# A V copy, a V cast and the folding of two weight matrices reordered, in a kernel of sliding-window attention and a multiplicative FFN

## The chip, the cores and the metric

The kernel runs on one core of one Trainium2 chip. The metric is the device time of one execution in microseconds (us), median of several runs. The engines are named as in the profile: PE (matmuls; PEld is its loading of weights), DVE (vector), ACT (scalar), POOL (GpSimd) and SP (which here only issues DMAs). POOL issues DMAs too, between its own instructions.

## What is computed

q, k and v are (8 batches, 8 heads, 576 positions, 64), fp32. Attention is causal with a window of 64 positions; its output, 4608 tokens of 512 values, goes through an FFN that multiplies two projections and has two output matrices with nothing between them:

```python
scores = scale * np.matmul(q, k.transpose(0, 1, 3, 2))
mask = (rel >= 0) & (rel < window)          # rel = query - key, window = 64
attn = softmax(where(mask, scores, -1e9))
x = (attn @ v).transpose(0, 2, 1, 3).reshape(4608, 512)
a = x @ w1; b = x @ w2                      # 512 x 1024 each
out = (a * b @ w3) @ w_out                  # 1024 x 1024, then 1024 x 512
```

## The kernel before, in words

Everything is computed in fp16 with fp32 accumulation. The order of all instructions is written out by hand: each engine works through its own list in program order, and semaphores join the lists.

**Folding.** Since nothing stands between w3 and w_out, the kernel computes wc = w3 @ w_out once and uses that. w3 has eight row blocks of 128 (`fc` 0 to 7). `fold_t(fc)` (L487) turns one with eight PE transposes (L492) into a PSUM bank `f_ps`, and DVE copies it back over the block (L493). `fold_mm(fc, half, cp, nf)` (L495) multiplies `nf` turned blocks with one half (256 columns) of w_out, eight matmuls for each block (L501), and `cp` copies the result to `wc_sb` (L503). Blocks 0 to 3 lie in the tile `ab` and blocks 4 to 7 in a part of `xT` that the first batches don't use. Before, all first halves are done as their blocks are turned, and the second halves of two blocks at a time follow between the values of batch 0.

**Loads at the start.** q and k of batch 0 come through the queues of SP and ACT. All else is on POOL's queue, which converts to fp16 on the way: w3 in four pieces of two blocks (`load_w3(n)`, L482, 512 KB read each), w_out in two halves (`load_wo(half)`, L476, 512 KB each), V of batch 0 (`load_rows(0, "v")`, L217, two of 288 KB), then w1 and w2 in halves (L471), k and q of batch 1, and V of batch 1 in blocks (`load_v`, L241).

**V.** Batch 0's V comes in rows, is cast into another order in two halves (`cast_qk`, L226), transposed (`transposes`, L262 on PE with copies L266) and transposed back per block of keys (`keys_of_v`, L273 and L275). From batch 1 on V is loaded by blocks of 128 keys straight into `v16s[b % 2]`, blocks 0, 2, 3 and parts of 4 and 5; block 1 and half of 4 overlap others and are copied from them on DVE by `copy_v(b, c)` (L245, L247).

**Attention.** A batch has six steps d (three segments of 192 queries, two pairs of heads). `scores(d)` is 8 matmuls into the bank `s_ps` (L296), an exp on ACT (L300), and two masks on POOL (L308 and L310; four in the first segment). `values(d)` is 16 matmuls with V into `o_ps`, or into `s_ps` if that is given (L338; L354 from batch 2 on), a logarithm and an exp on ACT (L344, L345) for the reciprocal of the sums, and a multiply on DVE (L346) into `xT`. Batch 1's steps are d = 6 to 11.

**FFN.** `ffn_ab(g, fc)` is 16 matmuls of 128x512 into two banks `f_ps` (L432), a copy on ACT (L437) and a multiply on DVE (L438), for 512 tokens `g` and a column block `fc`. `ffn_o(g, t)` is eight matmuls with `wc_sb` for 128 tokens (L450), a copy on DVE (L452) and a store on SP's queue (L459). There are three `f_ps` banks, one `o_ps`, one `s_ps` (of two banks each) and one `tp`.

**The order around the change** is L540 to L660: loads, casts and transposes of batch 0, scores(0) to scores(5) among the first fold steps, V of batch 0, values(0) to values(5) among the other fold steps, then batch 1's k and q: cast (half on DVE, half on ACT) and transposed. From `ffn_ab(0, 0)` (L624) on, FFN work of the first 512 tokens stands between the steps of batch 1; POOL casts batch 2's k and q in the same stretch (L634, L638) and issues the loads of its V (L639, L651). From L676 on a planner places later work by due times; it isn't touched. `keep_busy(n)` (L523) is n matmuls without use.

Of the kernel before, what the change touches and what calls it, by code (L numbers as in the profile page):

```python
# [8 lines left out]
FP32 = mybir.dt.float32  # L9
# [6 lines left out]
P = 128  # L16
# [128 lines left out]
def kernel(  # L145
# [11 lines left out]
    nc = tc.nc  # L157
    B, H, S, D = q.shape
    N = B * S
    DM = H * D  # L160
# [52 lines left out]
    def load_rows(b, which):  # L213

        t = sb.tile([P, 2, TI * D], FP16, name="rows", bufs=3)
        for hh in range(2):
            nc.gpsimd.dma_start(out=t[:, hh], in_=big_rows(which, b, hh))  # L217
        raws[which, b] = t
# [6 lines left out]
    def cast_qk(b, which, hh, cp):  # L225
        cp(t16_of(b, which)[:, :, hh * D:hh * D + D], raws[which, b][:, hh].rearrange("p (i d) -> p i d", d=D))  # L226
# [16 lines left out]
    def copy_v(b, c):  # L243
        vh = v_heads(b)
        dve_cp(vh[0:D, c], vh[D:P, c - 1])  # L245
        if c == 1:
            dve_cp(vh[D:P, 1], vh[0:D, 2])  # L247
# [4 lines left out]
    def transposes(b, which, *cs, into=None, cps=None):  # L252

        t16 = t16s[which, b]
        if cs[0] == 0:
            turned[which, b] = sb.tile([P, NJ, S], FP16, name=which + "T", bufs=1 if which == "v" else 2)
        dst = turned[which, b]
        if into is None:
            into = [ps_t.tile([P, 6, P], FP16, name="tp")]
        for c, tp in zip(cs, into):  # L260
            for i in range(6):
                nc.tensor.transpose(tp[:, i, :], t16[:, 6 * c + i, :], ident16)  # L262
        if cps is None:
            cps = [dve_cp if which == "k" or c != 1 else act_cp for c in cs]
        for c, tp, cp in zip(cs, into, cps):
            cp(dst.rearrange("q j (p i) -> q j p i", i=TI)[:, :, :, 6 * c:6 * c + 6],  # L266
               tp.rearrange("q i (p j) -> q j p i", p=TP))

    def keys_of_v(b, js, into, cps):

        for j, tp in zip(js, into):
            for c in range(6):
                nc.tensor.transpose(tp[:, c, :], turned["v", b][:, j, VBLK[c]:VBLK[c] + P], ident16)  # L273
        for j, tp, cp in zip(js, into, cps):
            cp(v16s[b % 2][:, :, j].rearrange("p c (a e) -> p c a e", a=2)[:, :, :, 0:D],  # L275
               tp.rearrange("p c (a e) -> p c a e", a=2))
# [37 lines left out]
    def values(d, pool=None):  # L314
        b, r = divmod(d, 6)
        si, jp = divmod(r, 2)
        j0 = 2 * jp
        v16 = v16s[b % 2]
        pt = probs.pop(d)
        seg = SEGS[si]  # L320
        q_base = seg[0][1]
        o_ps = ps_v.tile([P, 2, 512], FP32, name="o_ps") if pool is None else \
            ps_s.tile([P, 2, 512], FP32, name="s_ps")
        if jp == 0:
            lns[b, si] = sb.tile([P, NJ, 192], FP32, name="ln_s", bufs=4)
        y = lns[b, si][:, j0:j0 + 2]
        r = sb.tile([P, 2, 192], FP32, name="r")
        x0 = (b * S + q_base) % RING
        xs = xT[:, j0:j0 + 2, x0:x0 + 192]
        if b < SHORT:  # L330

            for jj in range(2):
                c0 = 0
                for bi, (k0, q0, n, _) in enumerate(seg):
                    o0 = jj * 192 + q0 - q_base
                    for e in range(2):
                        for a in range(2):
                            nc.tensor.matmul(o_ps[a * D:a * D + D, e, o0:o0 + n],  # L338
                                             v16[:, si * 2 + bi, j0 + jj, (2 * a + e) * D:(2 * a + e) * D + D],
                                             pt[:, a, jj, c0:c0 + n],  # L340
                                             start=(jj == 0 and bi == 0), stop=(bi == 1), skip_group_check=True)
                    c0 += n
            o, total = (o_ps[:, e, 0:384].rearrange("p (j n) -> p j n", j=2) for e in range(2))
            nc.scalar.activation(y, total, AF.Ln)  # L344
            nc.scalar.activation(r, y, AF.Exp, scale=-1.0)  # L345
            nc.vector.tensor_tensor(xs, o, r, ALU.mult)  # L346
            return
        for jj in range(2):
            first = True
            for a in range(2):  # L350
                c0 = 0
                for bi, (k0, q0, n, _) in enumerate(seg):
                    o0 = a * 192 + q0 - q_base
                    nc.tensor.matmul(o_ps[:, jj, o0:o0 + n],  # L354
                                     v16[:, si * 2 + bi, j0 + jj, a * D:a * D + P],
                                     pt[:, a, jj, c0:c0 + n],
                                     start=first, stop=(bi == 1), skip_group_check=True)
                    first = False
                    c0 += n
        nc.scalar.activation(y[0:D], o_ps[D:P, :, 0:192], AF.Ln)  # L360
        nc.scalar.activation(y[D:P], o_ps[0:D, :, 192:384], AF.Ln)  # L361
        nc.scalar.activation(r, y, AF.Exp, scale=-1.0)  # L362
        nc.vector.tensor_tensor(xs[0:D], o_ps[0:D, :, 0:192], r[0:D], ALU.mult)  # L363
        nc.vector.tensor_tensor(xs[D:P], o_ps[D:P, :, 192:384], r[D:P], ALU.mult)  # L364
# [109 lines left out]
    def load_wo(half):  # L474
        cols = slice(half * 256, half * 256 + 256)
        nc.gpsimd.dma_start(out=wo16[:, :, cols], in_=moe_w_out[:, cols].rearrange("(e p) m -> p e m", p=P))  # L476
# [7 lines left out]
    def turned_w3(fc):  # L484
        return w3_rows(fc).rearrange("p a (e n) -> p (a e) n", n=P)

    def fold_t(fc, cp=dve_cp):  # L487

        w3 = turned_w3(fc)
        tp = ps_f.tile([P, 8, P], FP16, name="f_ps")  # L490
        for ec in range(8):
            nc.tensor.transpose(tp[:, ec, :], w3[:, ec, :], ident16)  # L492
        cp(w3, tp)  # L493

    def fold_mm(fc, half, cp, nf=1):  # L495

        cols = slice(half * 256, half * 256 + 256)
        o_ps = ps_f.tile([P, 2, 256], FP32, name="f_ps")
        for f in range(nf):
            for ec in range(8):  # L500
                nc.tensor.matmul(o_ps[:, f], turned_w3(fc + f)[:, ec, :], wo16[:, ec, cols],  # L501
                                 start=(ec == 0), stop=(ec == 7), skip_group_check=True)
        cp(wc_sb[:, fc:fc + nf, cols], o_ps[:, 0:nf])  # L503
# [19 lines left out]
    def keep_busy(n):  # L523

        d = ps_t.tile([P, P], FP32, name="tp")
        for _ in range(n):
            nc.tensor.matmul(d, ident16, ident16, start=True, stop=True)
# [13 lines left out]
    load_wo(0)  # L541
    load_w3(1)
    load_rows(0, "v")
    for n in range(2, 4):
        load_w3(n)
    load_wo(1)

    def bank(pool, name):

        t = pool.tile([P, 2, 1024] if name != "f_ps" else [P, 1, 1024], FP16, name=name)  # L550
        return t[:, 0, 0:768].rearrange("p (i n) -> p i n", i=6)

    def tp_bank():
        return ps_t.tile([P, 6, P], FP16, name="tp")
# [25 lines left out]
    fold_t(2)  # L580
    fold_t(3)
    scores(4)
    fold_mm(2, 0, act_cp)
    for hh in range(2):
        cast_qk(0, "v", hh, dve_cp)
    fold_mm(3, 0, act_cp)
    scores(5)
    load_rows(1, "q")
    for i in range(2):
        load_w12(i, 1)  # L590
    load_v(1, 0, 2, 3)
    keep_busy(6)
    transposes(0, "v", 0, 1, 2, into=[bank(ps_v, "o_ps"), tp_bank(), bank(ps_f, "f_ps")], cps=[dve_cp, act_cp, act_cp])
    fold_t(4)
    fold_t(5)
    keys_of_v(0, [0, 1, 2], [bank(ps_v, "o_ps"), tp_bank(), bank(ps_f, "f_ps")], [act_cp, dve_cp, dve_cp])
    fold_mm(4, 0, act_cp)
    keys_of_v(0, [3], [tp_bank()], [dve_cp])
    fold_t(6)
    fold_mm(5, 0, act_cp)  # L600
    values(0)
    fold_t(7)
    fold_mm(6, 0, act_cp)
    values(1, ps_s)
    fold_mm(7, 0, act_cp)
    values(2)
    fold_mm(0, 1, dve_cp, 2)
    values(3, ps_s)
    fold_mm(2, 1, dve_cp, 2)
    values(4)  # L610
    fold_mm(4, 1, dve_cp, 2)
    values(5, ps_s)
    cast_qk(1, "k", 0, dve_cp)
    cast_qk(1, "k", 1, act_cp)
    load_v(1, 4, 5)
    fold_mm(6, 1, dve_cp, 2)
    cast_qk(1, "q", 0, dve_cp)
    cast_qk(1, "q", 1, act_cp)
    for n in range(3):
# [13 lines left out]
    for hh in range(2):  # L633
        cast_qk(2, "k", hh, pool_cp)  # L634
    ffn_ab(0, 4)
    scores(8)
    for hh in range(2):
        cast_qk(2, "q", hh, pool_cp)  # L638
# [3 lines left out]
    for d in range(6, 12):  # L642
        steps.pop(0)()
        store()
        if d in (6, 8):
            copy_v(1, {6: 1, 8: 4}[d])
        if d < 9:
            scores(d + 3)
        values(d, ps_s if d in (9, 11) else None)
        if d == 6:  # L650
            load_v(2, 4, 5)  # L651
        if d > 8:
            transposes(2, "k", d - 9)
# [76 lines left out]
```

## Time and profile before

| what | value |
|---|---|
| median of 6 runs | 291.99 us (291.1 to 292.8) |
| the profiled execution | 293.7 us |
| its span, first to last instruction | 292.0 us |
| PE / PEld busy | 276.2 us (95%) / 161.4 us (55%) |
| DVE / ACT / POOL busy | 180.2 (62%) / 170.0 (58%) / 179.1 (61%) |
| granted TensorE clock, mean | 0.998 |
| POOL's DMA queue (software_dynamic) | 38960 packets, 38.1% of 16 engines |

All of the stages share the 292 us, so a share of busy time says little about one of them. A timeline lists instructions of one engine, neighbours of one line merged: start and duration in us, engine, line, operation, output<-inputs, shape, count, and in brackets the idle time of the engine ahead of it with what ended it. The releaser is inferred: among several things waited for, it is the one that ended last.

### The profile page before, as it was taken

How to read it: one execution, taken by the hardware profiler on the slowest of the kernel's cores; microseconds unless marked ns; L12 is line 12 of the kernel's file. 1: busy time of each engine (PE TensorE's matmuls, PEld its weight loads, DVE VectorE, ACT ScalarE, POOL GpSimd, SP SyncE). 2: the span in 40 equal slices, each digit the busy share in tenths (PEclk: the TensorE clock that was granted, in tenths of full speed). 3: DMA queues.
4: the chain of work that ended last, by engine and by line, in shares of the span. 5: the costliest groups of instructions: out<-in, count | busy, mean ns of one | idle time of the engine just before them, and what ended most of it. 6: DMA issues, size and time to landing. Idle time of an engine off the chain costs nothing.

```text
span 292.0 us, 6234 instructions
## 1 busy us (share of the span) xinstructions
PE 276.2 (95%) x2425; PEld 161.4 (55%) x2425; DVE 180.2 (62%) x277; ACT 170.0 (58%) x281; POOL 179.1 (61%) x214
## 2 busy tenths in 40 slices
PE   7789999978998999999999999999999999999992
PEld 7668775434554555555555787455555445444441
DVE  0557456356767568687687856587867555555531
ACT  2656556664566746866776565487568765641300
POOL 8789830799469948695779363786596444402200
PEclk9999999999999999999999999999999999999999
DMA  6999999919297939094739560950094011002013
GB/s 244 222 211 204 210 205 149 399 33 112 106 334 177 64 143 327 4 113 130 311 25 126 168 237 0 168 62 2 36 154 41 2 73 73 2 36 109 2 39 112
DMA packets 48449, 37.68 MB, mean 129 GB/s; under 512 B 34160, under 2 KB 38512, under 8 KB 48416
## 3 DMA queue, kind: packets, MB, share of 16 engines
q0 software_dynamic: 38960, 11.14, 38.1%
q1 hardware_dynamic: 9024, 24.79, 23.3%
q10 hardware_dynamic: 432, 1.31, 1.3%
q8 instruction: 20, 0.33, 0.4%
q14 instruction: 13, 0.11, 0.1%
HBM read 38.80 MB, written 9.44 MB: 165 GB/s over the span
## 4 chain that ended last, share of the span: by engine, by line
PE 77%; POOL 9%; DMA 5%; ACT 4%; DVE 2%; issue 1%; SPq 0%; POOLq 0%; ACTq 0%
PE f_ps L432 36%; PE f_ps L450 20%; PE o_ps L354 5%; PE tp L262 5%; PE s_ps L296 4%; PE f_ps L501 4%; DMA ab<-in_moe_w_out_dram 3%; DMA stage<-in_q_dram 2%; POOL pt L310 2%; POOL pt L308 2%; POOL v L536 2%; POOL q L226 1%; ACT pt L300 1%; POOL v L241 1%; PE s_ps L338 1%
## 5 line engine op out<-in xcount | busy, mean ns | idle before, releaser
L432 PE MATMUL f_ps<-xT,w_sb 128*128 128x512 f16 (+1 forms) x640 | 134.2, 358 | 0.0
L308 POOL TENSOR_SCALAR_AFFINE_SELECT pt<-pt 128x512 f16<-128x512 f16 (+1 forms) x64 | 52.4, 819 | 69.7 <-ACT pt L300 69.7
L432 PEld LDWEIGHTS <-w_sb 128*128 128x128 f16 x640 | 59.7, 98 | 50.3 <-issue 0.3
L450 PE MATMUL f_ps<-wc_sb,ab 128*128 128x512 f16 (+1 forms) x296 | 66.9, 373 | 0.1
L438 DVE TENSOR_TENSOR ab<-f_ps,a_sb 128x512 f16<-128x512 f32 x72 | 49.8, 691 | 22.9 <-PE f_ps L432 21.1
L300 ACT ACTIVATE pt<-s_ps 128x1024 f16<-128x1024 f32 (+1 forms) x48 | 45.7, 952 | 23.8 <-PE s_ps L296 22.3
L437 ACT COPY a_sb<-f_ps 128x512 f32<-128x512 f32 x72 | 41.7, 579 | 24.8 <-PE f_ps L432 23.9
L310 POOL TENSOR_SCALAR_AFFINE_SELECT pt<-pt 128x512 f16<-128x512 f16 (+1 forms) x64 | 51.9, 811 | 4.5
L363 DVE TENSOR_TENSOR xT<-o_ps,r 64x384 f16<-64x384 f32 x36 | 19.8, 550 | 40.8 <-ACT r L362 40.8
L450 PEld LDWEIGHTS <-ab 128*128 128x128 f16 x296 | 27.6, 98 | 27.6 <-issue 0.3
L360 ACT ACTIVATE ln_s<-o_ps 64x384 f32<-64x384 f32 x36 | 17.5, 487 | 33.3 <-PE o_ps L354 33.3
L452 DVE COPY t2k<-f_ps 128x512 f32<-128x512 f32 (+1 forms) x36 | 24.5, 682 | 10.9 <-PE f_ps L450 10.4
L241 POOL DMA_DIRECT2D v<-in_v_dram x35 | 29.6, 853 | 2.2 <-DMA rows<-in_k_dram 1.0
L354 PEld LDWEIGHTS <-v 128*128 128x128 f16 x288 | 18.2, 98 | 9.5 <-ACT pt L300 0.8
L354 PE MATMUL o_ps<-pt,v 128*128 128x128 f16 (+1 forms) x288 | 20.8, 215 | 1.2 <-POOL pt L310 1.2
L296 PEld LDWEIGHTS <-kT 64*128 64x128 f16 x384 | 10.7, 94 | 18.1 <-issue 16.9
L364 DVE TENSOR_TENSOR xT<-o_ps,r 64x384 f16<-64x384 f32 x36 | 20.2, 561 | 0.5
L362 ACT ACTIVATE r<-ln_s 128x384 f32<-128x384 f32 x36 | 18.8, 522 | 1.1
L296 PE MATMUL s_ps<-qT,kT 64*128 64x128 f16 (+1 forms) x384 | 18.2, 214 | 0.4
L266 DVE COPY kT<-tp 128x768 f16<-128x768 f16 x19 | 18.1, 950 | 0.0
L361 ACT ACTIVATE ln_s<-o_ps 64x384 f32<-64x384 f32 x36 | 17.4, 482 | 0.4
L226 POOL CAST k<-stage 128x1152 f16<-128x1152 f32 x12 | 13.7, 1147 | 1.7 <-PE tp L262 1.7
(86 smaller groups left out, 234.2 us busy)
## 6 DMA issues: line engine op xcount, KB each, us to landing
out_dram<-t2k SPq DMA_DIRECT2D x35, 256.0 KB
stage<-in_k_dram SPq DMA_DIRECT2D x13, 576.0 KB
stage<-in_q_dram SPq DMA_DIRECT2D x13, 576.0 KB
v<-in_v_dram POOLq DMA_DIRECT2D x28, 128.0 KB, 4.5
w_sb<-in_moe_w_dram POOLq DMA_DIRECT2D x4, 512.0 KB, 12.6
ab<-in_moe_w_dram POOLq DMA_DIRECT2D x2, 512.0 KB, 8.6
ab<-in_moe_w_out_dram POOLq DMA_DIRECT2D x2, 512.0 KB, 13.5
xT<-in_moe_w_dram POOLq DMA_DIRECT2D x2, 512.0 KB, 15.1
```

What stands on the lines that cost most here:

```text
L241: nc.gpsimd.dma_start(out=vh[lo:P, c], in_=v[b, :, s0:s0 + P - lo, :].rearrange("h s d -> s h d"))
L296: nc.tensor.matmul(s_ps[:, a, jj, c0:c0 + n], kT[half, j, k0:k0 + P], qT[half, j, q0:q0 + n], start=True, stop=True, skip_group_check=True)
L300: nc.scalar.activation(pt[:, :, :, 0:w], s_ps[:, :, :, 0:w], AF.Exp, bias=-SHIFT, scale=scale)
L308: nc.gpsimd.affine_select(out=sl, in_=sl, pattern=pat, compare_op=ALU.is_ge, fill=0.0, base=off, channel_multiplier=-1)
L310: nc.gpsimd.affine_select(out=sl, in_=sl, pattern=[[-s, m] for s, m in pat], compare_op=ALU.is_ge, fill=0.0, base=63 - off, channel_multip ...
L354: nc.tensor.matmul(o_ps[:, jj, o0:o0 + n], v16[:, si * 2 + bi, j0 + jj, a * D:a * D + P], pt[:, a, jj, c0:c0 + n], start=first, stop=(bi = ...
L364: nc.vector.tensor_tensor(xs[D:P], o_ps[D:P, :, 192:384], r[D:P], ALU.mult)
L432: nc.tensor.matmul(d[:, f * n + c0:f * n + c1], w[:, dc, (fc + f) * P:(fc + f + 1) * P], xT[:, dc, xc:xc + c1 - c0], start=first, stop=(dc ...
L437: act_cp(a_sb[:, 0:nf * n], a_ps[:, 0:nf * n])
L438: nc.vector.tensor_tensor(ab[:, fc:fc + nf, lo:hi], b_ps[:, 0:nf * n].rearrange("p (f n) -> p f n", f=nf), a_sb[:, 0:nf * n].rearrange("p ...
L450: nc.tensor.matmul(o_ps[:, 0:c1 - c0], ab[:, fc, t * P:t * P + P], wc_sb[:, fc, c0:c1], start=(fc == 0), stop=(fc == 7))
L452: cp(o_sb[:, c0:c1], o_ps[:, 0:c1 - c0])
```

## The change

Three groups of edits, all in the order written out by hand.

1. `copy_v(1, 1)` moves from behind ffn_ab(0, 5) to behind ffn_ab(0, 4), ahead of scores(8).
2. V of batch 0: half 0 is cast on DVE as before, half 1 on ACT instead of DVE, and `keep_busy(6)` ahead of its transposes goes. The copies of fold_mm(2, 0) and fold_mm(3, 0) move from ACT to DVE, behind the casts.
3. The second half of w_out is loaded ahead of w3's last two pieces. Blocks 0 to 3 are folded in halves as before, but their second halves stand earlier, among V's transposes. Blocks 4 to 7 are folded at full width by a new function, `fold_full`: eight matmuls of 128x512 and one copy in place of two times eight of 128x256. The places of fold_t(4) to fold_t(7) move, and no fold step stands behind values(5) any more.

```diff
+    def fold_full(fc, cp):
+
+        o_ps = ps_f.tile([P, DM], FP32, name="f_ps")
+        for ec in range(8):
+            nc.tensor.matmul(o_ps, turned_w3(fc)[:, ec, :], wo16[:, ec, :], start=(ec == 0), stop=(ec == 7))
+        cp(wc_sb[:, fc, :], o_ps)
+
...
     load_rows(0, "v")
+    load_wo(1)
     for n in range(2, 4):
         load_w3(n)
-    load_wo(1)
...
     scores(4)
-    fold_mm(2, 0, act_cp)
-    for hh in range(2):
-        cast_qk(0, "v", hh, dve_cp)
-    fold_mm(3, 0, act_cp)
+    cast_qk(0, "v", 0, dve_cp)
+    cast_qk(0, "v", 1, act_cp)
+    fold_mm(2, 0, dve_cp)
+    fold_mm(3, 0, dve_cp)
     scores(5)
...
-    keep_busy(6)
     transposes(0, "v", 0, 1, 2, into=[bank(ps_v, "o_ps"), tp_bank(), bank(ps_f, "f_ps")], cps=[dve_cp, act_cp, act_cp])
+    fold_mm(0, 1, dve_cp, 2)
+    keys_of_v(0, [0, 1, 2], [bank(ps_v, "o_ps"), tp_bank(), bank(ps_f, "f_ps")], [act_cp, dve_cp, dve_cp])
     fold_t(4)
+    keys_of_v(0, [3], [tp_bank()], [dve_cp])
+    fold_mm(2, 1, act_cp, 2)
+    values(0)
     fold_t(5)
-    keys_of_v(0, [0, 1, 2], [bank(ps_v, "o_ps"), tp_bank(), bank(ps_f, "f_ps")], [act_cp, dve_cp, dve_cp])
-    fold_mm(4, 0, act_cp)
-    keys_of_v(0, [3], [tp_bank()], [dve_cp])
+    fold_full(4, dve_cp)
+    values(1, ps_s)
+    fold_full(5, dve_cp)
     fold_t(6)
-    fold_mm(5, 0, act_cp)
-    values(0)
+    values(2)
     fold_t(7)
-    fold_mm(6, 0, act_cp)
-    values(1, ps_s)
-    fold_mm(7, 0, act_cp)
-    values(2)
-    fold_mm(0, 1, dve_cp, 2)
     values(3, ps_s)
-    fold_mm(2, 1, dve_cp, 2)
+    fold_full(6, dve_cp)
     values(4)
-    fold_mm(4, 1, dve_cp, 2)
+    fold_full(7, dve_cp)
     values(5, ps_s)
     cast_qk(1, "k", 0, dve_cp)
     cast_qk(1, "k", 1, act_cp)
     load_v(1, 4, 5)
-    fold_mm(6, 1, dve_cp, 2)
     cast_qk(1, "q", 0, dve_cp)
...
     ffn_ab(0, 4)
+    copy_v(1, 1)
     scores(8)
...
-        if d in (6, 8):
-            copy_v(1, {6: 1, 8: 4}[d])
+        if d == 8:
+            copy_v(1, 4)
```

## The prediction

> **What bounds the kernel now.** I read the page first: PE is busy 95% of the span and DVE, ACT and POOL about 60% each, so a gain must be a hole in PE's row, and a hole counts only if nothing behind it is late as well. So I went to the places where PE stands still in the two stretches that the change edits: folding w3 and w_out (16.7 to 43.7 us) and the first FFN stage (43.7 to 89.5). In the order of PE's timeline:
>
> ```profile
> 23.17 0.51 PE L527 MATMUL tp<-ident 128*128 128x128 f16 x6
> ...
> 26.17 0.51 PE L273 MATMUL o_ps<-ident,vT 128*128 128x128 f16 x6 [0.39 <-ACT vT L266]
> ...
> 32.67 1.05 PE L501 MATMUL f_ps<-ab,xT 128*128 128x256 f16 x8 [0.44 <-DVE xT L493]
> ...
> 40.91 0.64 PE L338 MATMUL s_ps<-pt,v 128*64 128x128 f16 x16
> 41.48 1.92 PE L501 MATMUL f_ps<-ab,xT 128*128 128x256 f16 x16
> 43.74 0.50 PE L262 MATMUL o_ps<-ident,k 128*128 128x128 f16 x6 [0.34 <-ACT k L226]
> ...
> 60.19 0.43 PE L338 MATMUL o_ps<-pt,v 128*64 128x64 f16 x12 [2.15 <-DVE v L247]
> ...
> 68.27 0.64 PE L338 MATMUL s_ps<-pt,v 128*64 128x128 f16 x16 [0.22 <-POOL pt L310]
> ...
> 72.08 0.64 PE L338 MATMUL o_ps<-pt,v 128*64 128x128 f16 x16 [1.01 <-DVE t2k L452]
> ```
>
> Start, duration, and in brackets the idle time and its releaser. The change aims at three of these holes (0.39, 0.44 and 2.15 us) and at a filler (L527). Below I measure PE from start to start of its groups, because the ends of matmuls overlap what follows by about 0.1 us; so measured, the holes at 26.17, 32.67 and 43.74 are 0.52, 0.50 and 0.41 us.
>
> The last two rows matter most. In POOL's timeline behind them, from the first mask of batch 1 on:
>
> ```profile
> 52.36 0.63 POOL L308 TENSOR_SCALAR_AFFINE_SELECT pt<-pt 128x512 f16<-128x512 f16 x1 [12.13 <-ACT pt L300]
> ...
> 56.66 2.23 POOL L226 CAST k<-stage 128x1152 f16<-128x1152 f32 x2
> 58.85 1.15 POOL L308 TENSOR_SCALAR_AFFINE_SELECT pt<-pt 128x1024 f16<-128x1024 f16 x1
> 60.06 1.10 POOL L310 TENSOR_SCALAR_AFFINE_SELECT pt<-pt 128x1024 f16<-128x1024 f16 x1
> 61.11 2.23 POOL L226 CAST q<-stage 128x1152 f16<-128x1152 f32 x2
> 63.28 2.65 POOL L241 DMA_DIRECT2D v<-in_v_dram  x3
> 65.92 1.13 POOL L308 TENSOR_SCALAR_AFFINE_SELECT pt<-pt 128x1024 f16<-128x1024 f16 x1
> 67.12 1.09 POOL L310 TENSOR_SCALAR_AFFINE_SELECT pt<-pt 128x1024 f16<-128x1024 f16 x1
> ```
>
> No row after the first has an idle time: POOL is busy without a hole from 52.36 to 74.24. Its masks for scores(9) end at 68.21 and for scores(10) at 72.03, just when PE starts values(9) and values(10); the releaser named at 72.08 (a copy ending at 72.04, which values(10) doesn't read) only ended 0.01 us later. From 51 to 72 us POOL sets the end, not PE. From 72.08 to 88.08 PE has no hole.
>
> **Step 1: copy_v(1, 1) sooner.** Two DVE copies (L245 0.72, L247 1.07 us), no DMA, no added instruction. They stand one slot earlier, behind the multiply of ffn_ab(0, 4) that ends at 56.13, not behind that of ffn_ab(0, 5) at 58.28. What they read landed by 48.3 (V blocks issued at 33.8 and 35.24, landing 13.2 and 13.0 us later). They end near 58.0 before the shift of step 4; values(6) is due at 57.74, so of the 2.15 us PE keeps about 0.2. Queued behind them on DVE is the multiply of ffn_ab(0, 5), 0.4 us later; its PSUM bank is needed again only by ffn_ab(0, 7), some 2 us on. Then PE runs 2 us ahead, does values(6) to values(8) and ffn_o(0, 0), and stops at values(9), whose mask POOL still ends at 68.21. The wait moves to 68.27 and grows there from 0.22 to about 2.3 us. **Worth at the end: 0.** POOL's list is the same, and it gets no earlier unless scores(6) does.
>
> **Step 2: the fold, to the start of transposes(1, "k") (43.74).** Terms start to start, changes only:
> - keep_busy(6) goes: −0.54 (23.17 to 23.71). V's second half is now cast on ACT, behind exp(4): 22.07 plus 1.14 (ACT's row of this shape at 42.55) plus 0.06 to PE gives 23.27, so 0.10 of it becomes a wait: **−0.44**. DVE's cast of half 0 ends at 22.38 as before. exp(5), behind the ACT cast, starts at 23.28 in both; the copies of fold_mm(2) and (3) go to DVE, whose 0.9 us hole before 24.25 hides them.
> - The wait for vT at 26.17 goes, as fold_mm(0, 1) now stands there: **−0.52**. The one at 32.67 (a w3 copy queued on DVE behind a values multiply) goes too: **−0.50**. Next late is fold_full(5): its fold_t(5) copy ends near 32.9, PE comes at 33.2.
> - Rows 4 to 7 at full width: before, first halves 0.87+0.96+0.97+0.98 and second halves 2x1.85, 7.48 in all. A 128x512 group of eight took 1.81 ahead of values (73.00 to 74.81) and 1.73 ahead of transposes (75.73 to 77.46); three of one and one of the other make 7.16: **−0.32**. That fold_mm(0, 1) stands ahead of transposes and fold_t(6), (7) ahead of values gives −0.12 and +0.07: **−0.05**.
> - w_out's second half: DMA issues are moved on POOL's queue, none added, and they end at the same 12.6 us. V's rows landed at 21.91, then w3 2.48 and 2.51 us later each, w_out's half after 2.64 (11.64 plus 17.9, 29.54). In the new order the half lands at 24.55; PE, through with V's transposes at 24.28, waits **+0.27**. The w3 pieces land at 27.05 and 29.54, needed at 27.3 and 34.9: hidden. keys_of_v(3) waits 0.03 for a bank.
> - **The tail.** In before, values(5) starts at 40.91 and the k transposes 2.83 us later, because they wait for work queued on ACT behind values(5):
>
> ```profile
> 41.59 0.49 ACT L344 ACTIVATE ln_s<-s_ps 128x384 f32<-128x384 f32 x1 [1.38 <-PE s_ps L338]
> 42.12 0.52 ACT L345 ACTIVATE r<-ln_s 128x384 f32<-128x384 f32 x1
> 42.55 1.14 ACT L226 COPY k<-rows 128x1152 f16<-128x1152 f16 x1
> ```
>
> There fold_mm(6, 1) covered 1.85 of it, leaving 0.41 idle. After the change nothing of the fold stands behind values(5); ACT's three instructions are the same, so PE idles 2.26: **+1.85**, which gives back most of what was saved above.
>
> Sum: −0.44 −0.52 −0.50 −0.32 −0.05 +0.27 +0.03 +1.85 = **+0.32 us**; the transposes start at 44.06. The terms saved were real work or waits, but the fold's last piece was the cover of an ACT chain, and it is gone.
>
> **Step 3: what the rest makes of it.** ffn_ab(0, 0) to scores(6) have no hole in before and follow 0.32 later; POOL's run and values(10) too, and the q load that SP issues behind the stores at 79.05 and that POOL's cast at 86.14 waits for.
>
> **Step 4: sum.** The profiled execution took 293.7 us, span 292.0; by this it would be 294.0 and 292.3. The median shown, 291.99, lies 1.7 below that execution; moved by the same 0.32 it gives **292.3**.
>
> **Unknowns.** The w_out half in its new place: its wait is 0 if it lands by 24.28 and 1.12 if it takes what the first half took (13.13 to 16.62, 3.49); I take 2.64, the same transfer with the same queue behind it: −0.27/+0.85. The ACT cast lies between DVE's 0.45 alone and 1.35 beside POOL: −0.10/+0.21. The four wide groups may lose the 0.08 of their hand-over three times: −0.24. DVE copies beside POOL: a mask took 1.31, not 1.10, beside L226 at 23.3, but the POOL cast beside L245 at 58.31 kept its 1.14; I take 0, from 0 to +0.4 on POOL's run, and nothing below, since its rows beside L245 and L247 are within 0.05 of the others.
>
> [...] After the 2.15 us hole at 58 the next eight matmuls took 1.90, as before it, and the page's granted clock stays 9. [...] Beside POOL's work the two copies of 64x512 took 0.72 and 1.07, against 0.29 at 79.65. [...]
>
> **Rivals.** (a) The 2.15 us come off the end, since the waits list them as PE's longest in this stretch: 291.99+0.32−2.15 = 290.2. Against it stands POOL's unbroken row; it needs POOL to get quicker by itself. 0.11. (b) Slower: the w_out half lands as late as the first did, at 25.40. It decides from 24.28 on, one for one, because from there to values(5) PE's list has no other hole: +1.17, 293.2. For it: PE waited 0.66 on the first half at 16.66. Against: that one shared the engines with the q and k loads before 10 us. 0.17. (c) The change doesn't do what it says: the copies stretch to 1.1 each beside POOL's casts and values(6) still waits up to 0.7. That costs nothing while POOL decides: 292.3, inside the forecast.
>
> **Chances.** The forecast with (c), 291.4 to 292.9: 0.68. Rival (b) 0.17, (a) 0.11, and 0.04 for POOL's run stretched beyond 0.55. A measurement of this kernel can tell about 0.3%, 0.88 us: same 0.68, faster 0.11, slower 0.21. The range leaves out (a) and the far end of (b): from 292.3 less 0.61 for the three downward bounds and 0.4 for the spread of the runs (291.1 to 292.8), to 293.3.
>
> **What would show it.** PE's row named L247 at 60.19 gone or under 0.7; a new wait for POOL at values(9) of 2 us or more; PE idle about 2.3 us ahead of the k transposes, released by ACT's k cast; a wait of about 0.3 for w_out near 24.5; scores(6) at 51.3. The prediction is wrong if POOL's run from the first batch-1 mask to the scores(10) mask isn't 19.7 us long, or if the k transposes start far from 44.1.

## The result, and the profile after

The changed kernel takes 294.55 us, median of 33 runs (292.22 to 296.21); the kernel before, run beside it, 292.42 (70 runs, 290.77 to 295.86). The ratio is 1.0064, 95% interval 1.0049 to 1.0079: 1.9 us slower (1.4 to 2.3), where 0.3 us slower was forecast. (The two medians lie 2.1 apart; the text goes by the ratio.)

The profiled execution after took 294.77 us, its span is 292.9. The two spans differ by 0.96 us only, because the profile after was better off elsewhere. Its first fold_mm started 0.93 us earlier (15.73, w_out's first half having landed sooner). From values(12) to the last matmul it took 0.98 less, with 0.64 more behind that: there POOL's cast of q at 86.37 waited 0.16 us for its load, where before's at 86.14 waited 1.24, and PE waits at values(13) for the masks behind that cast. Of the other profiles, e6 has 1.6 us of this wait, e8 0.6 and the rest none; whether the change has a part in it isn't shown. So I compare distances along PE's list, not times from the start. In us, start to start, in the two profiles and those of the runs below (each column begins where the one before it ends):

| kernel | first fold_mm to k transposes | to scores(6) | to values(10) | ratio to before (95%) |
|---|---|---|---|---|
| before | 27.08 | 7.29 | 21.04 | 1 |
| after | 27.61 | **8.98** | 21.06 | 1.0064 (1.0049 to 1.0079) |
| e1_fill_k | 28.30 | 7.29 | 21.69 | 1.0025 (1.0000 to 1.0050) |
| e2_fill_both | 27.61 | 7.29 | 21.06 | 0.9995 (0.9975 to 1.0016) |
| e3_copy_alone | 26.88 | 7.29 | 21.06 | 0.9990 (0.9969 to 1.0012) |
| e4_fold_alone | 27.60 | 7.29 | 21.05 | 1.0050 (1.0024 to 1.0076) |
| e5_full7_last | 25.74 | 7.29 | 21.66 | 0.9977 (0.9955 to 1.0000) |
| e6_tail_alone | 29.06 | **8.97** | 21.31 | 1.0065 (1.0038 to 1.0091) |
| e7_short_hole | 27.79 | 7.29 | 21.40 | 1.0006 (0.9984 to 1.0027) |
| e8_before_fill | 26.87 | 7.29 | 21.05 | 0.9984 (0.9955 to 1.0013) |
| e9_early_cast | 25.24 | 7.99 | 21.06 | 0.9990 (0.9966 to 1.0014) |
| e10_early_cast_pool | 25.34 | 7.99 | 19.55 | 0.9925 (0.9900 to 0.9950) |
| e11_cover_and_pool | 25.14 | 7.29 | 19.56 | **0.9891** (0.9868 to 0.9913) |
| e12_old_fold | 26.38 | 7.29 | 19.55 | 0.9923 (0.9895 to 0.9951) |

The first column of after is the late start that the prediction worked out, somewhat larger. The second is the surprise: from the k transposes to scores(6), where nothing in the list changed, 1.69 us more. (The 28.30 of e1 has another cause, in the last section.) PE's timeline after, at the tail of the fold (start, duration, engine, line, operation, shapes, count, idle time ahead):

```profile
40.52 0.64 PE L338 MATMUL s_ps<-pt,v 128*64 128x128 f16 x16
43.34 0.50 PE L262 MATMUL o_ps<-ident,k 128*128 128x128 f16 x6 [2.19 <-ACT k L226]
...
44.35 5.30 PE L432 MATMUL f_ps<-xT,w_sb 128*128 128x512 f16 x16
49.49 0.50 PE L262 MATMUL o_ps<-ident,q 128*128 128x128 f16 x6
```

The hole (a stretch in which PE is idle) ahead of the k transposes is there as forecast, released by ACT's k cast. But the sixteen matmuls of ffn_ab(0, 0) and (0, 1) take 5.14 us to the start of the next group (44.35 to 49.49). Before they took 3.46 (44.75 to 48.21):

```profile
44.75 3.62 PE L432 MATMUL f_ps<-xT,w_sb 128*128 128x512 f16 x16
48.21 0.50 PE L262 MATMUL o_ps<-ident,q 128*128 128x128 f16 x6
```

No wait is named. The view by windows shows why. Its columns are the window, the busy time of PE, PEld, DVE, ACT and POOL (instructions), then the granted TensorE clock, the DMA share and GB/s:

```profile
41.13:44.55 3.42, 1.23 (x21) 1.12 (x20) 1.81 (x5) 3.32 (x5) 0.00 (x0) 1.00 1.60 189
44.55:47.96 3.41, 3.41 (x9) 1.18 (x8) 1.58 (x3) 1.08 (x2) 0.00 (x0) 0.50 3.33 126
47.97:51.38 3.41, 3.41 (x31) 2.10 (x30) 2.16 (x4) 1.94 (x3) 0.00 (x0) 1.00 0.60 95
```

In the middle one the clock is 0.50 and PE, though busy throughout, does 9 matmuls. The clock was halved for exactly these 3.41 us, which at half speed lose 1.7. The 3.41 us before them hold the whole hole: PE idle 3.42 − 1.23 = 2.19.

In the fold, PE's row for the new wait for w_out, which stands where the wait for vT and the filler were, and ACT's for the cast that PE waits for at 43.34:

```profile
23.69 1.92 PE L508 MATMUL f_ps<-ab 128*128 128x256 f16 x16 [0.22 <-DMA ab<-in_moe_w_out_dram]
```

```profile
41.20 0.49 ACT L344 ACTIVATE ln_s<-s_ps 128x384 f32<-128x384 f32 x1 [1.36 <-PE s_ps L338]
41.72 0.52 ACT L345 ACTIVATE r<-ln_s 128x384 f32<-128x384 f32 x1
42.15 1.14 ACT L226 COPY k<-rows 128x1152 f16<-128x1152 f16 x1
```

The three durations on ACT are those of before, with nothing on PE beside them. The moved copy did what step 1 said: the hole at values(6) is gone and stands at values(9), where POOL releases it.

```profile
59.03 0.54 PE L338 MATMUL o_ps<-pt,v 128*64 128x128 f16 x16
...
69.57 0.64 PE L338 MATMUL s_ps<-pt,v 128*64 128x128 f16 x16 [2.32 <-POOL pt L310]
...
73.39 0.64 PE L338 MATMUL o_ps<-pt,v 128*64 128x128 f16 x16 [1.01 <-DVE t2k L452]
```

The last masks ahead of these two, in POOL's timeline, end at 69.52 and 73.33:

```profile
68.42 1.10 POOL L310 TENSOR_SCALAR_AFFINE_SELECT pt<-pt 128x1024 f16<-128x1024 f16 x1
...
72.23 1.10 POOL L310 TENSOR_SCALAR_AFFINE_SELECT pt<-pt 128x1024 f16<-128x1024 f16 x1
```

POOL's run from its first batch-1 mask to the mask of scores(10) takes 19.68 us, 19.66 before.

### The profile page after: what moved, and what is told of

Read it like the earlier page. It is cut to its first block, busy times and chain, and to the rows that moved or that the text cites. A ratio compares the mean times of both kernels' runs of the same rounds, so it can differ in the third digit from the quotient of the medians.

```text
span 292.9 us, 6158 instructions
## 1 busy us (share of the span) xinstructions
PE 276.5 (94%) x2387; PEld 158.3 (54%) x2387; DVE 179.0 (61%) x279; ACT 169.0 (58%) x277; POOL 179.0 (61%) x214
## 4 chain that ended last, share of the span: by engine, by line
PE 77%; POOL 10%; DMA 6%; ACT 2%; DVE 2%; issue 1%; SPq 0%; POOLq 0%; ACTq 0%
PE f_ps L432 37%; PE f_ps L450 20%; PE o_ps L354 5%; DMA ab<-in_moe_w_out_dram 5%; PE tp L262 4%; PE s_ps L296 4%; PE f_ps L499 2%; DMA stage<-in_q_dram 2%; POOL pt L310 2%; POOL v L543 2%; POOL pt L308 2%; PE f_ps L508 1%; POOL q L226 1%; PE s_ps L338 1%; POOL v L241 1%
## 5 line engine op out<-in xcount | busy, mean ns | idle before, releaser
L432 PE MATMUL f_ps<-xT,w_sb 128*128 128x512 f16 (+1 forms) x640 | 135.9, 361 | 0.0
L452 DVE COPY t2k<-f_ps 128x512 f32<-128x512 f32 (+1 forms) x36 | 24.4, 681 | 11.0 <-PE f_ps L450 10.5
```

Of the source, the lines that this page charges most:

```text
L432: nc.tensor.matmul(d[:, f * n + c0:f * n + c1], w[:, dc, (fc + f) * P:(fc + f + 1) * P], xT[:, dc, xc:xc + c1 - c0], start=first, stop=(dc ...
L452: cp(o_sb[:, c0:c1], o_ps[:, 0:c1 - c0])
```

## The experiments

Theory A: the time after is the late start of the k transposes plus a clock that is halved, in some executions, behind PE's two holes of 2.19 and 2.32 us. Theory B: the halved clock is an accident of one profile, and lateness alone makes the 1.0064.

**e1_fill_k** and **e2_fill_both**: matmuls without use in the hole ahead of the k transposes; in the second kernel also in that ahead of values(9), by the lower edit.

```diff
+    keep_busy(36)
     transposes(1, "k", 0, 1, 2, into=three(), cps=[act_cp, dve_cp, dve_cp])
...
+        if d == 9:
+            keep_busy(36)
         values(d, ps_s if d in (9, 11) else None)
```

> The changed kernel with 36 matmuls without use (2.0 us) ahead of the k transposes, where PE otherwise stands still for 2.2 us. Theory A (clock): that hole lets the TensorE clock be halved for 3.41 us in many executions, 1.7 us each time; filled, the sixteen matmuls of ffn_ab(0, 0) and (0, 1) take 3.5 us from start to start and not 5.1, the k transposes still start 2.8 us behind values(5), and the ratio to before falls from 1.0064 to 1.001 to 1.004 (the hole ahead of values(9) is still open). Theory B (late work): the halved clock is an accident of one profiled execution, and the time is lost by the later start of what follows; filled or not, the ratio stays at 1.006.

> As the run before, and 36 more matmuls without use ahead of values(9), where PE waits 2.3 us for POOL. Theory A: no hole of 2 us is left, the mean granted clock is at least 0.995 in every execution, and the ratio is that of the predicted shift alone, 1.000 to 1.002. Theory B: 1.006.

Measured 1.0025 and 0.9995. Work that nobody needs made the kernel faster by 0.4% and then by another 0.3%, with the k transposes still 2.83 us behind values(5) in both: A, not B. One part of the forecast missed: the mean granted clock was to be at least 0.995 in every execution of e2, and in five of twelve it was 0.991 to 0.994. Where these lost it isn't recorded. In e2's profile the mean granted clock is 0.999 over 290.7 us, which is 0.6 us at half speed in all, less than one stretch of 3.41. In e1's it was halved at 70.4, behind the hole at values(9) that was left open, and to values(10) it took 21.69 and not 21.06: there a halved clock cost 0.6, since PE waits for POOL at values(10) in any case.

**e3_copy_alone** and **e4_fold_alone**: the kernel before with the moved copy, and the changed kernel without it.

> The kernel before with copy_v(1, 1) moved alone. The prediction's step 1: the hole moves from values(6) to values(9) and POOL's run from the first batch-1 mask to the mask of scores(10) stays 19.7 us, so the end doesn't move: ratio 0.999 to 1.002. Theory A says the same, unless a hole of 2.3 us halves the clock more often than one of 2.15 us: up to 1.003. If the removed wait came off the end: 0.993.

> The changed kernel with copy_v(1, 1) back in its old place, so the cast and the fold order alone. Theory A: the hole ahead of the k transposes is there, 1.003 to 1.006, the clock halved behind it in about half of the executions or more. Theory B: the shift of the transposes by 0.3 to 0.5 us alone, 1.001 to 1.002, the rest of the 1.0064 then belonging to the moved copy.

0.9990 and 1.0050. The copy alone gains nothing that the runs can tell (2.15 us would have been 0.993), and the fold order costs the time: B's 1.001 to 1.002 lies outside e4's interval. The prediction's rival (a) is out. In e4's profile the clock was not halved, although the hole is as long as in after. The view by windows shows the difference, the next window's clock standing in the second row:

```profile
41.77:45.18 3.41, 1.55 (x21) 1.31 (x22) 1.97 (x4) 3.38 (x5) 0.00 (x0) 1.00 1.85 177
45.18:48.59 3.41, 3.41 (x24) 1.77 (x22) 2.07 (x5) 1.32 (x3) 0.00 (x0) 1.00 3.08 97
```

The window began inside the hole and holds 1.86 us of it. Within the profiles the recorded changes of the clock lie whole multiples of 3.413 us apart: in after's the clock is halved from 44.55, full from 47.97 and halved again from 290.31, 1 and 71 windows later; in e6's it is halved from 46.51 and from 63.58, 5 windows apart; in e1's from 12.37 and from 70.40, 17 windows. Where this grid falls differs from profile to profile: counted from the start of the span, the halved windows stand 0.18 us behind a multiple of 3.413 in after, 1.15 in e7 (69.42), 2.14 in e6 and 2.67 in e5 (67.52).

**e5_full7_last**: the cover (work for PE while the ACT chain runs) given back.

```diff
-    fold_full(7, dve_cp)
     values(5, ps_s)
     cast_qk(1, "k", 0, dve_cp)
     cast_qk(1, "k", 1, act_cp)
     load_v(1, 4, 5)
+    fold_full(7, dve_cp)
     cast_qk(1, "q", 0, dve_cp)
```

> The changed kernel with fold_full(7) behind values(5), where fold_mm(6, 1) stood before: the ACT chain has its cover back. Theory A (late work and a halved clock, both from the uncovered 2.2 us): from the first fold_mm to the k transposes 25.8 us and not 27.6, no halved clock behind them, so the ratio falls by 1.8 us and by the half of the executions that lose 1.7 us, 2.6 us in all: 0.996 to 0.999. Theory B (late work alone): 1.8 us less, 1.000 to 1.001.

0.9977 (0.9955 to 1.0000), inside A's band and below B's, which begins where the interval ends; 25.74 us to the k transposes as forecast, and 0.87% less than after, 2.5 us, of which lateness is 1.87.

**e6_tail_alone**: the cover taken from before.

```diff
+    fold_mm(6, 1, dve_cp, 2)
     values(5, ps_s)
     cast_qk(1, "k", 0, dve_cp)
     cast_qk(1, "k", 1, act_cp)
     load_v(1, 4, 5)
-    fold_mm(6, 1, dve_cp, 2)
```

> The kernel before with fold_mm(6, 1) moved ahead of values(5) and nothing else: the cover taken away alone. Theory A: 1.85 us of late work and the halved clock in about half of the executions, 2.6 us: 1.008 to 1.010. Theory B: 1.85 us, 1.0055 to 1.007.

1.0065 (1.0038 to 1.0091): this ratio doesn't decide; it lies in B's band, and A's begins inside its interval. The profile does show the halved clock, twice, behind the k transposes' hole and behind before's own hole at values(6):

```profile
43.09:46.50 3.41, 1.22 (x21) 1.12 (x20) 1.80 (x5) 3.28 (x5) 0.00 (x0) 1.00 2.59 149
46.51:49.92 3.41, 3.41 (x9) 1.22 (x8) 1.55 (x3) 1.11 (x2) 0.00 (x0) 0.50 1.85 45
60.17:63.58 3.41, 1.27 (x21) 0.58 (x21) 2.48 (x3) 1.38 (x2) 3.34 (x4) 1.00 0.41 155
63.58:66.99 3.41, 3.41 (x20) 1.36 (x18) 0.56 (x1) 1.60 (x3) 3.41 (x4) 0.50 0.01 2
```

The first cost 1.68 us (8.97 for 7.29). The second cost 0.27 (21.31 for 21.04), for POOL decides when values(10) starts.

**e7_short_hole**: as e1 with 10 matmuls in place of 36.

> The changed kernel with only 10 matmuls without use (0.56 us) ahead of the k transposes, so that the hole is cut from 2.2 to about 1.65 us. If the clock is halved when PE idles for more than about 2 us within one window of 3.41 us, as the windows of the profiled executions so far say (1.86 not halved, 2.07 and 2.19 halved), this is as good as filling the hole: 1.001 to 1.004, no halved clock there. If any hole does it in proportion to its length: 1.005 to 1.006.

1.0006 (0.9984 to 1.0027), just under the forecast 1.001 to 1.004, which the interval overlaps; the rival's 1.005 to 1.006 lies outside the interval. Ten matmuls without use, 0.56 us, are as good as 36: the cleanest evidence, since the k transposes start no sooner than in after. PE's timeline and two pairs of windows:

```profile
41.40 0.73 PE L534 MATMUL tp<-ident 128*128 128x128 f16 x10
43.66 0.50 PE L262 MATMUL o_ps<-ident,k 128*128 128x128 f16 x6 [1.53 <-ACT k L226]
...
44.66 3.62 PE L432 MATMUL f_ps<-xT,w_sb 128*128 128x512 f16 x16
```

```profile
42.12:45.53 3.41, 1.88 (x24) 1.42 (x24) 2.29 (x5) 3.24 (x4) 0.00 (x0) 1.00 1.81 180
45.53:48.94 3.41, 3.41 (x28) 2.00 (x27) 2.07 (x4) 1.46 (x3) 0.00 (x0) 1.00 3.17 106
66.01:69.42 3.41, 1.23 (x24) 1.01 (x24) 0.71 (x2) 0.52 (x2) 3.34 (x4) 1.00 1.41 154
69.42:72.83 3.41, 3.41 (x18) 1.23 (x18) 1.80 (x3) 0.49 (x1) 3.34 (x4) 0.50 0.91 58
```

Behind 1.53 us idle the clock stays 1.00; at values(9), behind 2.18 us in one window, it is 0.50 in the next.

**e8_before_fill**: before, with `keep_busy(36)` ahead of values(6).

> The kernel before with 36 matmuls without use ahead of values(6), into its own 2.15 us hole. Theory A: this hole halves the clock in about half of the executions as well, but what follows it waits for POOL at values(9) and values(10) anyway, so that only about 0.5 us of each 1.7 reaches the end: 0.998 to 1.000. If the whole 1.7 us counted: 0.997. If before never loses its clock there: 1.000.

0.9984 (0.9955 to 1.0013). All three bands touch the interval: whether before loses time at its own hole stays open from this run; e6's 0.27 us for one halving there says that it is little. That before loses its clock there in some executions is likely all the same: the mean granted clock is 0.9907 over the 35 executions of before beside this run, and 0.9953 over the twelve with the hole filled.

**e9_early_cast**: batch 1's k is cast ahead of values(4) and (5), on DVE, so that ACT's list behind values(5) no longer stands ahead of the k transposes.

```diff
     fold_full(6, dve_cp)
+    for hh in range(2):
+        cast_qk(1, "k", hh, dve_cp)
     values(4)
     fold_full(7, dve_cp)
     values(5, ps_s)
-    cast_qk(1, "k", 0, dve_cp)
-    cast_qk(1, "k", 1, act_cp)
     load_v(1, 4, 5)
...
-    transposes(1, "k", 0, 1, 2, into=three(), cps=[act_cp, dve_cp, dve_cp])
+    transposes(1, "k", 0, 1, 2, into=[bank(ps_v, "o_ps"), tp_bank(), bank(ps_f, "f_ps")], cps=[act_cp, dve_cp, dve_cp])
```

> The changed kernel with both casts of batch 1's k on DVE behind fold_full(6), ahead of values(4) and values(5), and the k transposes into banks that values(5) doesn't hold. The ACT chain behind values(5) no longer stands ahead of them: from values(5) to the k transposes 0.6 us and not 2.8, from the first fold_mm to them about 25.4; ffn_ab(0, 0) may wait some 0.3 us for the multiply of values(5). No hole of 2 us is left in the fold, one of about 2.3 stays ahead of values(9). Theory A: 1.2 us less than before, 0.994 to 0.998. If the end were set elsewhere: 1.000.

0.9990 (0.9966 to 1.0014), above the band, which its interval overlaps, and near the 1.000 of the other case: by itself it decides nothing. The k transposes stand 0.57 us behind values(5). ffn_ab then waited twice, for the multiply of values(5) and for a copy, 0.70 together and not 0.3.

**e10_early_cast_pool**: e9, and a second half each of batch 2's k and q cast on DVE.

```diff
-    for hh in range(2):
-        cast_qk(2, "k", hh, pool_cp)
+    cast_qk(2, "k", 0, pool_cp)
...
-    for hh in range(2):
-        cast_qk(2, "q", hh, pool_cp)
+    cast_qk(2, "q", 0, pool_cp)
...
+        if d == 7:
+            cast_qk(2, "k", 1, dve_cp)
         if d == 8:
             copy_v(1, 4)
+            cast_qk(2, "q", 1, dve_cp)
```

> As the run before, and the second halves of batch 2's k and q cast on DVE instead of POOL, so that POOL's run from the first batch-1 mask to the mask of scores(10) is two casts of 1.14 us shorter, 17.4 us and not 19.7. If that run is what took the moved copy's 2.15 us back, from scores(6) to values(10) should now be about 18.9 us and not 21.0, no hole of 2 us is left on PE, and the ratio is 0.985 to 0.990. If not, no more than the run before.

0.9925 (0.9900 to 0.9950), short of the forecast 0.985 to 0.990, but 0.65% below e9: POOL's run was the bound. It takes 18.17 us, 19.68 in e9, and values(10) follows: 19.55 behind scores(6) and not 21.06 (18.9 was forecast). The hole at values(9) is 1.06 us, 2.57 in e9. So 1.5 us of the 2.28 taken off POOL are gained. POOL's timeline says where most of the rest went: the mask beside DVE's q cast (62.54 to 64.14) took 1.51, where its like takes 1.10, and its three DMA issues took 2.91, not 2.65.

```profile
62.39 1.13 POOL L308 TENSOR_SCALAR_AFFINE_SELECT pt<-pt 128x1024 f16<-128x1024 f16 x1
63.59 1.51 POOL L310 TENSOR_SCALAR_AFFINE_SELECT pt<-pt 128x1024 f16<-128x1024 f16 x1
```

**e11_cover_and_pool** and **e12_old_fold**: e10 with fold_full(7) behind values(5) as in e5; and e10's casts and copy in the load and fold order of before.

> As e10_early_cast_pool, with fold_full(7) behind values(5) as well: its 1.8 us then cover the multiply of values(5), which ffn_ab(0, 0) waited for. The same matmuls on PE, 0.4 to 0.7 us of waits between the first fold_mm and scores(6) gone, 33.3 to about 32.7 us: ratio 0.988 to 0.992.

> The kernel before with the moved copy, the early casts of k on DVE and the halves of batch 2's casts on DVE, as in e10, but with the load order, V cast and fold order of before. It says what the new fold is worth once its tail is mended: from the first fold_mm to scores(6) about 33.7 us against 32.7 in the run beside it, so a ratio about 0.003 above that of the run beside it, 0.992 to 0.996. If the new fold is worth nothing: the same ratio.

0.9891 and 0.9923, both as forecast. e11 beats both kernels, by 1.1% and 1.7%. From the first fold_mm to scores(6) it takes 32.43 us against e12's 33.67: with its tail mended, the new fold is worth about 1.2 us in the profiles and 0.3% of time, as forecast; with six runs each the two intervals overlap, so the 0.3% isn't shown by the times alone. PE's timeline of e11 at the tail has no hole left:

```profile
38.87 0.61 PE L338 MATMUL s_ps<-pt,v 128*64 128x128 f16 x16
39.41 1.90 PE L499 MATMUL f_ps<-ab,xT 128*128 128x512 f16 x8
41.15 0.50 PE L262 MATMUL o_ps<-ident,k 128*128 128x128 f16 x6
```

## Why the prediction was wrong, point by point

**What held.** Step 1: values(6) doesn't wait, values(9) waits 2.32 us (2.3 forecast), POOL's run is unchanged, the copy alone gives 0.9990. Within step 2: V's transposes start 0.49 us earlier after the first fold_mm than in the profile before (−0.44 forecast); w_out's second half landed 7.91 us behind the first fold_mm (7.89 forecast) and PE waited 0.39 for it (0.27), so rival (b) didn't come; the tail from values(5) to the k transposes is 2.82 (2.83), and 2.19 of it idle.

**What was a little off.** The late start came to +0.53 us against the profile before, and to +0.73 against e3 and e8, which have the same fold as before and took 0.2 less than that profile. Forecast was +0.32. From V's transposes to the k transposes after took 21.06, my terms give 20.79: 0.12 is the wait for w_out, 0.06 the four wide groups (7.22 for 7.16), and the last 0.09 I didn't trace. The 0.2 is the scatter of one profile, on which I had built the comparison.

**The step that failed** is the one that priced the new holes, 2.26 and about 2.3 us, at nothing beyond their own length; no run shows that price as one that holds in every execution. What the runs showed in its place: the clock was halved for the 3.41 us behind such a hole in some of the profiles, which cost 1.69 us behind the k transposes' hole (after) and 0.3 to 0.6 behind the one at values(9) (e7, e5 and e1). The one row for the price was before's hole of 2.15 us, behind which eight matmuls took their usual 1.90. It was a true reading of one execution, in which the grid (before's clock is halved from 290.69, 67 windows behind 61.99) cut the hole in two:

```profile
58.58:61.99 3.41, 1.80 (x19) 1.02 (x20) 1.78 (x3) 1.66 (x4) 3.34 (x4) 1.00 0.10 39
61.99:65.40 3.41, 3.41 (x43) 1.58 (x40) 1.52 (x4) 2.62 (x5) 3.41 (x5) 1.00 0.13 8
```

Only 1.61 us of idle time fell into one window. e6 has the same hole in the same place with 2.14 in one window, and there the clock was halved. Over the profiles, idle time of PE in one window and the next window's clock, between the fold and the first FFN stage's end:

| idle us in the window | next clock | kernels |
|---|---|---|
| 1.53, 1.61, 1.81, 1.86 | 1.00 | e7, before, e3, e4 |
| 2.14, 2.18, 2.19, 2.19 | 0.50 | e6, e7, after, e6 |
| 2.32, 2.33 | 0.50 | e5, e1 |

So in these rows the limit lies between 1.86 and 2.14; near the end of e4's span 2.07 us in one window, too, had a halved one behind it (e4's mean clock of 0.994 is 3.5 us at half speed in all). An estimate from these rows: with a limit of 2.0, between the two, a hole of 2.19 us on a grid of 3.41 that falls anywhere reaches it in (3.41 + 2.19 − 4.0) / 3.41 = 47% of executions, and one of 2.32 in 51%. Then after loses 0.47 x 1.69 behind the k transposes' hole and 0.51 x 0.6 at values(9), 1.1 us; before loses some 0.1 at its own. With the late start of 0.53 to 0.73 that makes 1.5 to 1.7; measured 1.9 (1.4 to 2.3). The mean granted clock of the 35 recorded executions of after runs from 0.981 to 0.997, and the highest clocks go with the shortest spans. How often each hole halves the clock wasn't counted: one profile for each kernel shows one place of the grid. The mean clocks allow a rough count: 0.988 over after's 35 executions and 0.996 over e2's twelve, a difference of 1.4 halved windows in each execution, where my estimate has 0.98. So the clock may well have the larger share, and how the 1.9 us split between clock and late start isn't shown: e2, whose k transposes start as late as after's, is no slower than before.

## What to carry to other kernels

Work that stands behind a step covers the chain that follows it (1.85 of 2.26 us in before): before moving it forward, see which engine's list the next PE work waits for, and move that wait (here the k cast) first. Here a wait removed upstream of an engine whose list has no hole only moved down to where that engine is waited for (the 2.15 us at values(6) became 2.32 at values(9), with POOL's run at 19.68 us; e3's ratio is 0.9990), until work was taken off it (e10, 0.9925). Where a kernel behaves like this one, in which 2.14 to 2.33 us of idle time in one window stood ahead of a halved clock, price a new PE hole of that size at its own length plus the chance of 3.41 us at half speed (1.69 us in after), and read several executions, since one profile shows one place of the grid.

## What the runs showed of the hardware that I had not expected

- In the stretch from 40 to 100 us the clock was halved behind 2.14 to 2.33 us of idle time in one 3.41 us window, and behind none of the 1.53 to 1.86 us in the table. In the first 13 us, among transposes and fillers, it was halved behind 1.68 (e1, e6) and 1.90 us (e5), and not behind 1.67 (e7). The mean clocks of these profiles (e1 0.982, e6 0.983, e5 0.986, e7 0.994) are 10.5, 10.0, 8.1 and 3.5 us at half speed, of which the halved windows of the later stretch hold 3.41, 6.83, 3.41 and 3.41. So 1.68 stood there ahead of a halved clock and 1.86 later ahead of a full one: PE's idle time alone doesn't tell, and what differs is open. In e1 the clock stayed halved for 6.83 us, which delayed its V transposes by 1.1 us (7.64 for 6.56 behind the first fold_mm).
- The moved copies of 64x512 took 0.29 and 0.39 us (57.44 to 58.15, beside POOL's last two small masks and the start of its k cast), where before they took 0.72 and 1.07 beside the cast and the masks behind it. In e10 a DVE cast of 128x1152 took 0.80 us beside the end of POOL's cast and its DMA issues, and 1.60 beside two POOL masks, of which the second took 1.51, not 1.10. The times differed with what stood beside them; no run took one pair alone, so what stretched them isn't shown.
